# First nine units of a 7-product matrix stage in plain 8-product form, with its preparation rearranged

## The chip, the cores and the metric

One Trainium2 chip, one core. The metric is the time of one execution on the device in microseconds (us). TensorE (PE) multiplies; VectorE (DVE), ScalarE (ACT) and GpSimd (POOL) do elementwise work; SyncE (SP) issues nearly all DMAs of the part that matters here. Each engine runs its own instructions in program order and waits on semaphores for the others.

## The reference, cut to what matters

Attention for 32 heads feeds a mixture of eight experts; its output `x` (2304 tokens, 512 features) goes through a normed gated layer with 1536 hidden columns:

```python
def _moe2_ref(x, w_gate, w_val, w_out, rms_g):
    rms = np.sqrt(np.mean(x * x, axis=-1, keepdims=True) + 1e-06)
    xn = x / rms * rms_g
    g = xn @ w_gate
    silu = g * (1.0 / (1.0 + np.exp(-g)))
    val = xn @ w_val
    return (silu * val @ w_out).astype(np.float32)
```

The change is in the part that computes `silu * val`. The weights of this layer arrive as 64-bit floats.

## The kernel before, in words

Every product of float32 matrices is made of three passes (`PASSES`, L762): each operand is split into a high part, cast by ScalarE to a rounded format, and a low part, the rest, subtracted by VectorE or GpSimd. A product `x @ w` is hi.hi + hi.lo + lo.hi.

**The stages.** Attention comes first, then `moe` (L868): experts s = 0 to 7, each with `gemm1` (L765, eight blocks f) and `gemm2` (L781, four blocks c). Then `glu` (L1245) computes silu(g) times val, and `glu_rest` (L1421) multiplies by `w_out` (the "go" products, L1393).

**The 7-product stage.** The tokens are taken in pairs of groups of 384: p = 0, 1, 2 stands for groups 2p and 2p+1. The weights are taken in 12 blocks f of 128 hidden columns, gate and value together. For one (p, f), called a unit, the 2 x 2 block product (two token groups by gate and value, over two halves of the 512 features) is computed with seven block products in Winograd's form rather than eight: sums of x blocks (S1 to S4) and of weight blocks are made beforehand, and sums of the products afterwards. A block product is six matmuls of 128 x 384 (two 128-row chunks, three passes). Products accumulate in three PSUM banks of the unit, `a`, `b` and `e`; the steps in `glu_step` (L1128) are u1 (copy of a), u2 (b + u1), u3 (b + u1 after the next product was added to b), c21, c12, c22, and then for each token group a sigmoid, `gate` (times g) and `h` (times val), and a store of h (`keep0`, `keep1`). c22, gate2 and h2 are GpSimd's.

**Preparation of a weight block** f: two loads into staging tiles (`w_load`), ten decode steps that turn 64-bit floats to float32 (`decoding`, L1051: VectorE with one ScalarE step), four sums (`w_sum`, GpSimd except for block 1), four casts (`w_cast`, L1097, ScalarE) and four subtractions (`w_rest`, L1102, GpSimd) into one of two buffers `ws0`, `ws1`. **Preparation of the x blocks** of a pair p: two loads from the DRAM array `ytd`, to which the experts' normed outputs are stored, into a staging tile (`glu_load`, L1012; `ringa` for p = 0 and 2, a tile `gx2a` for p = 1), four sums in place (`x_sum`, L1025, VectorE), seven casts (`x_cast`, L1029) and seven subtractions (`x_rest`, L1034) into `gx0a`, `gx0b` and so on.

**What sets the order.** Each engine's order is written out by hand. The first two weight blocks and the x blocks of p = 0 are prepared by `glu_head` (L1170), a generator of which `moe` takes one step after each block of the last experts' products, from the first block of expert 6's `gemm2` on; its instructions stand in each engine's queue between those of the experts. `moe`'s own work in that stretch is: a ReLU per block of `gemm1` on ScalarE (L777) and its residual on VectorE (L778), copies and squares per block of `gemm2` on ScalarE (L796 to L801), sums of squares on VectorE (L802), and `finish` (L813), the norm: a matmul with ones, a square root, a reciprocal (L819) and four multiplications (L822). For expert 7, `finish` is `k.tail`, put into the first unit. From `glu` on, a list `plan` of (due time in products, function) is sorted and emitted: products, unit steps, and the rest of the preparation at `slots`, fixed offsets within each unit (`ONDVE`, `ONPOOL`).

**Addresses.** `glu_first` (L990) opens a pool in the place of the pool that held the weights of the even experts and expert 7's transposed input, in the order ws0, ws1, gx0a, gx0b, ringa; a tile must wait for the last reader of what lay at its address. `glu_second` (L1001) opens the other pool in the place of expert 7's weights and hidden values.

## Time and profile before

| what | value |
|---|---|
| time, median of three runs | 947.37 us (946.16 to 947.95) |
| the profiled execution's own time | 947.75 us |
| its span, first to last instruction | 946.0 us |
| TensorE busy | 857.6 us (91%) |
| VectorE, ScalarE, GpSimd busy | 555.1, 471.8, 554.3 us |
| granted clock of TensorE, mean | 0.97 of full |

The profile takes one execution. Its page shows busy time of each engine, the span in 40 slices, the chain of work that ended last, and groups of instructions; the trace behind it can be asked for stretches of time, waits, single lines and the timeline. In a timeline, "[4.47 <-DMA ringa<-ytd]" means that the engine was idle for 4.47 us before this instruction and that a DMA into ringa ended the wait.

### The profile page before, as it was taken

To read this page: it belongs to the slowest core of one execution; us is meant where nothing else is said; L and a number is where in the kernel's file an instruction comes from. 1 tells how busy PE (TensorE), PEld (TensorE's weight loads), DVE (VectorE), ACT (ScalarE), POOL (GpSimd) and SP (SyncE) were. 2 spreads that over 40 slices of the span, in tenths; PEclk is the share of its full clock that TensorE was granted. 3 is DMA by queue.
4 is the path that set the end of the run, shared out by engine and by line. 5 is a ranking of instruction groups with operands and counts; after the bars stand their busy time and mean duration, and the time that the engine had idled before them with its cause. 6 is when DMAs were issued, how large, how long until landed. Compare 5 with 4: busy or idle time off the path is not lost.

```text
span 946.0 us, 15623 instructions
## 1 busy us (share of the span) xinstructions
PE 857.6 (91%) x5468; PEld 753.7 (80%) x5468; DVE 555.1 (59%) x1179; ACT 471.8 (50%) x1114; POOL 554.3 (59%) x471
## 2 busy tenths in 40 slices
PE   6998989898999999996457899999999999999995
PEld 4676767678899999995457798999999998778884
DVE  5556765645525543466888878888888877700000
ACT  4986969672756555653344333333333443443210
POOL 2002420223686666672845697888888878789541
PEclk9999999998999999998788999999999999999999
DMA  8997775205476565674232041322223278260001
GB/s 266 304 300 221 215 213 169 90 24 173 141 236 196 180 180 180 197 212 135 67 117 102 34 125 64 99 95 102 99 96 126 95 256 295 103 267 34 34 34 37
DMA packets 59452, 139.89 MB, mean 148 GB/s; under 512 B 6960, under 2 KB 24395, under 8 KB 59363
## 3 DMA queue, kind: packets, MB, share of 16 engines
q1 hardware_dynamic: 56403, 129.26, 43.1%
q0 software_dynamic: 2912, 9.46, 2.6%
q8 instruction: 45, 0.74, 0.3%
q14 instruction: 44, 0.36, 0.1%
q10 hardware_dynamic: 48, 0.07, 0.0%
HBM read 103.85 MB, written 34.92 MB: 147 GB/s over the span
## 4 chain that ended last, share of the span: by engine, by line
PE 61%; DVE 20%; ACT 6%; issue 6%; DMA 3%; POOL 2%; SPq 0%; POOLq 0%; ACTq 0%; DVEq 0%
PE go L1393 11%; PE gg L1123 11%; PE g L794 9%; PE g L774 9%; PE pvy L353 5%; PE t L307 5%; PE s L262 4%; DVE raw L1055 4%; DVE raw L1063 2%; PE tl L381 2%; ACT raw L1056 2%; DVE raw L1062 1%; PE sm L275 1%; DVE raw L1061 1%; DVE u L1139 1%
## 5 line engine op out<-in xcount | busy, mean ns | idle before, releaser
L658 POOL TENSOR_TENSOR u<-raw,u 128x1024 fp32r<-128x1024 f32 x64 | 154.4, 2425 | 100.6 <-ACT u L657 100.5
L794 PE MATMUL g<-h,u 128*128 128x256 f32 (+7 forms) x768 | 112.9, 306 | 10.9 <-DVE h L778 6.0
L794 PEld LDWEIGHTS g<-h,u 128*128 128x128 f32 x768 | 107.0, 198 | 13.5 <-DVE h L778 7.6
L774 PE MATMUL g<-xt,u 128*128 128x256 f32 (+7 forms) x768 | 104.3, 295 | 0.0
L774 PEld LDWEIGHTS g<-xt,u 128*128 128x128 f32 x768 | 101.4, 188 | 0.8
L248 DVE CUSTOM_DVE_ANT_0 sc<-s,in 128x128 f32<-128x128 f32 (+3 forms) x128 | 58.1, 490 | 39.8 <-ACT vp L365 13.0
L288 ACT ACTIVATE p<-sc,nm 128x128 f32<-128x128 f32 (+3 forms) x128 | 71.7, 596 | 8.4 <-DVE nm L248 7.7
L235 POOL COPY in<-in 64x64 f32<-64x64 f32 x32 | 8.0, 251 | 115.0 <-PE sm L277 46.2
L1102 POOL TENSOR_TENSOR ws<-raw,ws 128x512 fp32r<-128x512 f32 (+1 forms) x48 | 67.1, 1416 | 6.3 <-ACT ws L1097 6.3
L1123 PE MATMUL gg<-gx1a,ws 128*128 128x384 f32 x288 | 58.8, 347 | 13.1 <-DVE u L1141 13.1
L657 ACT CAST u<-raw 128x1024 fp32r<-128x1024 f32 x64 | 67.6, 1056 | 2.1 <-DMA raw<-in_w 2.1
L340 ACT COPY pt<-t 128x512 f32<-128x512 f32 (+3 forms) x160 | 55.7, 473 | 21.6 <-PE t L307 20.9
L1398 DVE COPY raw<-go 128x256 f32<-128x256 f32 x1 | 0.4, 424 | 110.5 <-ACT raw L1397 110.5
L1123 PEld LDWEIGHTS gg<-gx1a,ws 128*128 128x128 f32 x288 | 51.2, 192 | 16.6 <-DVE u L1141 16.6
L1157 POOL TENSOR_TENSOR h<-u,h 128x384 f32<-128x384 f32 x36 | 45.7, 1271 | 28.8 <-ACT h L1155 28.8
L802 DVE TENSOR_TENSOR sq<-sq,sn 128x256 f32<-128x256 f32 (+6 forms) x21 | 13.9, 664 | 82.4 <-ACT sn L801 82.4
L1123 PE MATMUL gg<-gx0a,ws 128*128 128x384 f32 x288 | 57.3, 340 | 2.9 <-DVE u L1141 2.9
L307 PE MATMUL t<-ident,p 128*128 128x128 f32 x400 | 52.6, 276 | 6.2 <-ACT pt L340 2.6
L1123 PE MATMUL gg<-gx2a,ws 128*128 128x384 f32 x288 | 56.9, 341 | 0.5 <-DVE u L1141 0.5
L1056 ACT ACTIVATE raw<-raw 128x512 f32<-128x512 f32 x36 | 24.3, 674 | 60.9 <-DVE raw L1055 48.7
L1123 PEld LDWEIGHTS gg<-gx0a,ws 128*128 128x128 f32 x288 | 50.6, 190 | 4.5 <-DVE u L1141 4.2
L1155 ACT ACTIVATE h<-u 128x384 f32<-128x384 f32 x36 | 19.0, 527 | 70.6 <-DVE u L1153 70.6
(289 smaller groups left out, 2076.8 us busy)
## 6 DMA issues: line engine op xcount, KB each, us to landing
raw<-in_w SPq DMA_DIRECT2D x64, 512.0 KB, 4.4
hd<-h SPq DMA_DIRECT2D x72, 192.0 KB, 1.8
in<-cumd SPq DMA_DIRECT2D x30, 256.0 KB, 9.8
...
```

Source lines behind the costliest of these rows:

```text
L248: k.nc.vector.tensor_tensor_reduce(out=out, in0=ps, in1=bias, scale=-0.125, scalar=3e38, op0=ALU.add, op1=ALU.min, accum_out=accum)
L288: k.nc.scalar.activation(out, st.s[i, h][:, 0:w], AF.Exp, bias=st.nm[:, n:n + 1], scale=-1.0, accum_out=acc)
L307: nc.tensor.transpose(ps[:, off:off + 128], src[:, 128 * j:128 * j + 128], k.ident)
L340: nc.scalar.copy(b, a)
L353: nc.tensor.matmul(st.y[r, a - 64:512], st.v[:, h, j, :], k.pt[:, h, o:o + S - a], start=j == 0, stop=j == 4)
L657: nc.scalar.copy(w[:, :, 0, :], raw)
L658: nc.gpsimd.tensor_tensor(w[:, :, 1, :], raw, w[:, :, 0, :].bitcast(F32), op=ALU.subtract)
L774: nc.tensor.matmul(ps[:, 0:n], w[:, f % 4, a, 128 * kc:128 * kc + 128], x[b][:, kc, 0:n], start=kc == 0 and i == 0, stop=kc == 3 and i == 2)
L794: nc.tensor.matmul(ps[:, 0:n], w[:, f % 4, a, 128 * c:128 * c + 128], k.h[b][:, f, 0:n], start=f == 0 and i == 0, stop=f == 7 and i == 2)
L1102: k.nc.gpsimd.tensor_tensor(w[:, c, LO, :], src, plain(w[:, c, HI, :]), op=ALU.subtract)
L1123: k.nc.tensor.matmul(k.ps[u, bank], w[:, a, 128 * c:128 * c + 128], x[:, b, GT * c:GT * c + GT], start=j < 3 and c == 0 and n == 0, stop=c ...
L1393: k.nc.tensor.matmul(acc[g][t], c[:, a, cols], w[:, b, :], start=f == 0 and i == 0, stop=f == NF - 1 and i == 2)
```

## The change

The first nine units are computed with eight plain block products (`WHOLE`) into four banks, with no sums; the other 27 keep seven products, in another order (`SEVEN`, `WHENS`), where the last two products of a unit come after the first two of the next. The head prepares only the four x blocks of p = 0 and weight block 0 in plain form, and decodes block 1; the rest moves into the plan. Decoding has four steps instead of five. c22, the weight sums, part of `w_rest` and `wo_split` go to VectorE; the copy p5 goes. `ringa` lies right behind `ws0`, `ws1` at the end; there are three staging tiles for x. The steps of the plan get new due times: the preparation takes the slots `FILL` (VectorE) and `FILLP` (GpSimd) in order.

```diff
@@ -969,12 +969,22 @@
 XB = 2 * GT
 LO, HI = 1, 0
 A11, A12, A22, S1, S2, S3, S4 = range(7)
-PRODUCTS = (("a", A11, 0), ("b", S2, 4), ("e", S1, 3), ("a", A12, 1), ("b", S3, 5), ("e", S4, 2), ("b", A22, 6))
-UNITS = ([(0, 0), (0, 1), (1, 0), (2, 0), (1, 1), (2, 1)] + [(p, f) for f in range(2, NF - 2) for p in range(3)]
+A21 = S1
+PLAIN = ((0, 0), (0, 1), (1, 0), (1, 1), (2, 0), (2, 1), (0, 2), (1, 2), (2, 2))
+UNITS = (list(PLAIN) + [(p, f) for f in range(3, NF - 2) for p in range(3)]
          + [(0, NF - 2), (1, NF - 2), (0, NF - 1), (1, NF - 1), (2, NF - 2), (2, NF - 1)])
...
+WHOLE = tuple((n, *xw) for n, pair in (("c11", ((A11, 0), (A12, 1))), ("c12", ((A11, 3), (A12, 2))),
+                                       ("c21", ((A21, 0), (A22, 1))), ("c22", ((A21, 3), (A22, 2)))) for xw in pair)
+SEVEN = (("a", A11, 0), ("b", S2, 4), ("a", A12, 1), ("e", S1, 3), ("b", S3, 5), ("b", A22, 6), ("e", S4, 2))
+WHENS = ((0, 1, 4, 5, 6, 9, 10), (0, 1, 6, 4, 5, 7, 8))
+NP8 = len(PLAIN)
+START = [8 * u for u in range(NP8)] + [8 * NP8 + 7 * u for u in range(len(UNITS) + 1 - NP8)]
+FILL = ([s + o for s in START[:NP8] for o in (0.65, 1.2, 1.75, 2.2, 3.25, 4.65, 5.2, 5.75, 6.25, 7.25)]
+        + [s + o for s in START[NP8:] for o in (1.3, 1.9, 2.5, 3.65, 4.15)])
+FILLP = [s + o for s in START[:NP8] for o in (0.2, 2.2, 4.2, 6.2)] + [s + o for s in START[NP8:] for o in (0.05, 1.6)]
+STEPS7 = (("u1", 1.05), ("gate1", 5.7), ("u2", 4.6), ("sig1", 5.05), ("u3", 7.1), ("c22", 7.65), ("c21", 10.1),
+          ("sig2", 10.7), ("gate2", 11.45), ("c12", 12.1), ("h2", 12.5), ("h1", 13.25), ("keep1", 13.8), ("keep0", 14.0))
+STEPS8 = (("sig1", 2.05), ("gate1", 2.7), ("h1", 4.1), ("keep0", 4.8), ("sig2", 6.05), ("gate2", 6.7), ("h2", 8.1), ("keep1", 8.8))
...
@@ -989,10 +999,11 @@
 def glu_first(k):
     P = k.gpool
-    k.ws = [glu_tile(k, P, [7, 2, 256], f"ws{n}", F32R) for n in range(2)]
+    k.ws = [glu_tile(k, P, [7, 2, 256], "ws0", F32R)]
+    k.yb = [glu_tile(k, P, [4, XB], "ringa")]
     k.gx = {}
     x_tiles(k, P, 0)
-    k.yb = [glu_tile(k, P, [4, XB], "ringa")]
+    k.ws.append(glu_tile(k, P, [7, 2, 256], "ws1", F32R))
...
@@ -1001,8 +1012,21 @@
 def glu_second(k):
     P = k.hpool
     x_tiles(k, P, 1)
-    k.tmp = [{n: glu_tile(k, P, [GT], f"{n}{i}") for n in ("u1", "p5", "u2", "u3", "h1", "h2")} for i in range(2)]
-    k.yb += [glu_tile(k, P, [4, XB], "gx2a"), k.yb[0]]
+    k.hs = [glu_tile(k, P, [2, GT], f"hs{i}") for i in range(2)]
+    k.yb += [glu_tile(k, P, [4, XB], "tmp"), glu_tile(k, P, [4, XB], "gx2b")]
+    a = glu_tile(k, P, [4, 2, XB], "gx2a", F32R)
+    k.gx[2] = [a[:, n] for n in range(4)]
+
+
+def glu_again(k):
+    b = glu_tile(k, k.hpool, [3, 2, XB], "gx2b", F32R)
+    k.gx[2] += [b[:, n] for n in range(3)]
+    k.yb[2] = k.yb[0]
+
+
+def glu_third(k):
+    t = glu_tile(k, k.hpool, [8, GT], "tmp")
+    k.tmp = [{"u1": t[:, 4 * i], "u2": t[:, 4 * i + 1], "u3": t[:, 4 * i + 2]} for i in range(2)]
...
     def top():
-        V.scalar_tensor_tensor(low, high, 0xC0000000, low, op0=ALU.bitwise_and, op1=ALU.bitwise_or)
-        k.nc.scalar.activation(hf, hf, AF.Abs)
+        V.scalar_tensor_tensor(low, high, 0x80000000, low, op0=ALU.bitwise_and, op1=ALU.bitwise_or)
+        k.nc.scalar.activation(hf, hf, AF.Abs, scale=65536.0)
     return (
         lambda: V.tensor_scalar(low, low, 29, None, op0=ALU.logical_shift_right),
         top,
-        lambda: V.tensor_scalar(hf, hf, TINY, None, op0=ALU.max),
-        lambda: V.tensor_scalar(high, high, 3, 0x3FFFFFFF, op0=ALU.logical_shift_left, op1=ALU.bitwise_and),
-        lambda: V.tensor_tensor(high, high, low, op=ALU.bitwise_or),
+        lambda: V.tensor_scalar(hf, hf, 65536.0 * TINY, None, op0=ALU.max),
+        lambda: V.scalar_tensor_tensor(high, high, 3, low, op0=ALU.logical_shift_left, op1=ALU.bitwise_or),
     )
...
+ORDER = ((0, 0), (0, 1), (1, 0), (1, 1), (0, 2), (0, 3), (1, 2), (1, 3))
+
+
 def w_decode(k, f, n):
-    decoding(k, k.raw[f, n // 5])[n % 5]()
+    m, step = ORDER[n]
+    decoding(k, k.raw[f, m])[step]()
...
-    eng.tensor_tensor(out, a, b, op=ALU.subtract)
+    k.nc.vector.tensor_tensor(out, a, b, op=ALU.subtract)
 def w_piece(k, f, n):
     g, gl, v, vl = w_parts(k, f)
-    c = (slice(0, 2), slice(2, 3), slice(3, 5), slice(5, 7))[n]
...
-    bank, xi, wi = PRODUCTS[j]
-    if j < 3:
+    whole = u < len(PLAIN)
+    bank, xi, wi = (WHOLE if whole else SEVEN)[j]
+    first = (u, bank) not in k.ps
+    if first:
         k.ps[u, bank] = k.psum.tile([128, 512], F32, name=f"gg{k.uid()}", tag="b")[:, 0:GT]
...
+    elif what == "c22":
+        V.tensor_tensor(u3, e, u3, op=add)
+    elif what == "c21":
+        V.tensor_tensor(u1, b, u1, op=add)
+    elif what == "c12":
+        V.tensor_tensor(u2, e, u2, op=add)
...
-        G.tensor_tensor(t["h2"], t["u1"], t["h2"], op=mult)
+        (V if whole else G).tensor_tensor(h2, c21, h2, op=mult)
     elif what == "h2":
-        G.tensor_tensor(t["h2"], t["h2"], t["p5"], op=mult)
+        (V if whole else G).tensor_tensor(h2, c22, h2, op=mult)
...
     dec(5)
     w_cast(k, 0, 0)
-    w_rest(k, 0, 0)
+    yield
+    w_rest(k, 0, 0, G)
     yield
     dec(6)
     yield
...
     dec(7)
...
+    for n in (1, 4):
+        w_cast(k, 0, n)
+        w_rest(k, 0, n, G)
+    yield
+    dec(8)
+    yield
+    dec(9)
+    yield
+    yield
+    x_cast(k, 0, "A11")
+    x_cast(k, 0, "A12")
+    x_rest(k, 0, "A11", V)
+    dec(10)
+    yield
+    x_cast(k, 0, "A21")
+    x_rest(k, 0, "A12", V)
+    x_cast(k, 0, "A22")
+    dec(11, 12)
+    yield
+    x_rest(k, 0, "A21", V)
+    x_rest(k, 0, "A22", G)
+    dec(13)
+    yield
+    dec(14, 15)
...
+        whole = u < len(PLAIN)
+        when = range(8) if whole else WHENS[u == len(UNITS) - 1]
+        for j, at in enumerate(when):
+            add(START[u] + at, glu_product, k, u, j)
+        for what, at in STEPS8 if whole else STEPS7:
...
+            add(START[u] + at, glu_step, k, u, what)
...
+    sums, done = {}, {}
+    for g in (2, 3):
+        add(0.01 * g, glu_load, k, g)
+    for n in (0, 1, 4):
+        t = pfill(0)
+        add(t - 0.1, w_cast, k, 1, n)
+        add(t, w_rest, k, 1, n, G)
+    t = fill(1.9, 5)
+    add(1.6, k.tail)
+    for g in (4, 5):
+        add(8.0 + 0.1 * g, glu_load, k, g)
+    x_rests(1, (("A11", V), ("A12", V), ("A21", V), ("A22", G)), 8.1)
+    load, over, sent = {2: 0.5, 3: 6.5}, {}, {}
+
+    def w_made(f):
+        whole = (0, f) in PLAIN
         for m in range(2):
...
+            add(load[f] + 0.1 * m, w_load, k, f, m)
+        for n in range(8):
+            t = fill(load[f] + 6.0)
+            add(t, w_decode, k, f, n)
+        for n in range(0 if whole else 4):
+            t = fill(t)
+            add(t, w_sum, k, f, n)
+        sent[f] = t + 0.8
+
+    def w_split(f):
+        whole = (0, f) in PLAIN
+        end = last[f - 2] + 1
+        at = max(START[end] + (0.2 if (0, f - 2) in PLAIN else 4.0), sent[f])
+        t = v = at
+        for n, eng in ((0, V), (4, G), (1, V)) if whole else ((0, V), (2, G), (3, G), (1, V)):
+            if eng is V:
+                t = v = fill(v + 0.8)
+            else:
+                t = at = pfill(at + 0.8)
+            add(t - 0.8, w_cast, k, f, n)
+            add(t, w_rest, k, f, n, eng)
+        over[f] = max(at + 1.5, v + 0.8)
+        load[f + 2] = over[f]
+
+    w_made(2)
+    x_rests(2, (("A11", V), ("A12", G), ("A21", V), ("A22", V)), 19.0)
+    w_split(2)
+    w_made(3)
+    x_sums(0, ("S3", "S1", "S2", "S4"), 12.5)
+    x_rests(0, (("S2", G), ("S3", V), ("S4", V)), 12.0)
+    w_split(3)
+    x_sums(1, ("S3", "S1", "S2", "S4"), 24.0)
+    x_rests(1, (("S2", G), ("S3", V), ("S4", V)), 24.0)
+    w_made(4)
+    x_rests(0, (("S1", V),), START[7] + 1.1)
+    x_rests(1, (("S1", G),), START[8] + 1.1)
+    t = done[0, "S1"] + 1.0
+    add(t, glu_again, k)
+    for g in (4, 5):
+        add(t + 0.1 * g, glu_load, k, g)
+    t = done[1, "S1"] + 1.0
+    add(t, glu_third, k)
+    assert t < START[9] + 1.0
+    x_sums(2, ("S3", "S1", "S2", "S4"), done[0, "S1"] + 7.0)
+    x_rests(2, (("S2", V), ("S1", V), ("S3", G), ("S4", V)), START[9] + 1.2)
+    w_split(4)
+    w_made(5)
+    add(130.0, glu_ids, k)
+    add(150.0, glu_turn_ids, k)
...
-    k.nc.gpsimd.tensor_tensor(w[:, LO, :], hf, plain(w[:, HI, :]), op=ALU.subtract)
+    k.nc.vector.tensor_tensor(w[:, LO, :], hf, plain(w[:, HI, :]), op=ALU.subtract)
...
-    add(7 * 33 + 0.6, glu_regions, k, 0)
...
+    add(end - 14 + 3.6, glu_regions, k, 0)
     for n in range(3):
         for g in range(2):
-            add(7 * 33 + 0.7 + 3 * n, h_load, k, g, 4 * n, 4 if n < 2 else 3)
+            add(end - 14 + 3.7 + 1.5 * n, h_load, k, g, 4 * n, 4 if n < 2 else 3)
     for g in range(2):
-        add(7 * 34 + 6.5, h_load, k, g, NF - 1, 1)
-    add(7 * 34 + 0.6, glu_regions, k, 1)
+        add(end - 7 + 7.2, h_load, k, g, NF - 1, 1)
+    add(end - 7 + 3.6, glu_regions, k, 1)
     for f in range(WREADY):
-        add(7 * 34 + 0.9 + 2.2 * f, wo_split, k, f)
+        add(end - 7 + 3.9 + 1.7 * f, wo_split, k, f)
     for n in range(AHEAD):
-        add(7 * 34 - 1.0 + 2.1 * n, glu_split, k, n)
-    add(7 * 35 + 0.6, glu_regions, k, 2)
+        add(end - 7 + 0.5 + 2.3 * n, glu_split, k, n)
+    add(end + 3.6, glu_regions, k, 2)
```

## Rows read from the trace of the kernel before

**Rows 1.** TensorE in the 40 slices of the page, tenths busy (each 23.65 us).

```profile
PE   6998989898999999996457899999999999999995
```

**Rows 2.** Windows (length, busy PE, PEld, DVE, ACT, POOL, clock, DMA share, GB/s).

```profile
437.00:450.00 13.00, 5.58 (x24) 3.88 (x22) 7.16 (x12) 4.27 (x9) 2.04 (x2) 0.73 0.49 164
450.00:460.20 10.20, 10.18 (x75) 10.18 (x76) 9.34 (x7) 5.18 (x10) 10.12 (x7) 0.85 0.48 156
460.20:477.30 17.10, 1.68 (x9) 1.28 (x8) 13.33 (x14) 5.05 (x12) 12.10 (x9) 0.59 0.00 0
477.30:541.20 63.90, 47.20 (x216) 44.04 (x215) 57.09 (x70) 24.76 (x43) 34.52 (x24) 0.87 0.27 94
541.20:781.40 240.20, 229.86 (x1294) 223.95 (x1294) 198.46 (x287) 93.31 (x191) 202.80 (x175) 1.00 0.34 115
781.40:946.00 164.60, 152.17 (x650) 120.91 (x648) 35.49 (x43) 49.20 (x101) 104.23 (x99) 0.99 0.30 114
```

**Rows 3.** TensorE's waits, 438 to 560 (total us, times, longest).

```profile
PE ms L816 <- DVE y L802: 15.4, 1, 15.4
PE gg L1123 <- DVE u L1141: 8.6, 4, 3.6
```

**Rows 4.** Timeline at the last expert (start, us, engine, line).

```profile
428.49 8.64 PE L774 MATMUL g<-xt,u 128*128 128x248 f32 x72
...
431.19 0.36 SPq L1043 DMA_DIRECT2D raw<-in_wv  x1
...
431.75 0.67 ACT L1097 CAST ws<-raw 128x512 fp32r<-128x512 f32 x1 [2.29 <-DVE raw L1063]
431.96 1.81 DVE L819 RECIPROCAL sq<-sq 128x268 f32<-128x268 f32 x1
...
433.81 1.72 DVE L822 SCALAR_TENSOR_TENSOR y<-y,gv,sq 128x268 f32<-128x268 f32 x4
...
437.16 1.31 SPq L1014 DMA_DIRECT2D ringa<-ytd  x2
...
442.27 0.83 ACT L1029 CAST gx0a<-ringa 128x768 fp32r<-128x768 f32 x1 [4.47 <-DMA ringa<-ytd]
443.00 0.37 ACT L777 ACTIVATE h<-g 128x248 fp32r<-128x248 f32 x1
```

**Rows 5.** Timeline of TensorE in the steady stretch, two products each.

```profile
637.04 2.26 PE L1123 MATMUL gg<-gx2a,ws 128*128 128x384 f32 x12
639.13 2.26 PE L1123 MATMUL gg<-gx2b,ws 128*128 128x384 f32 x12
```

**Rows 6.** Window of three units in the steady stretch.

```profile
634.84:658.04 23.20, 22.28 (x127) 21.77 (x127) 19.09 (x29) 8.88 (x18) 20.09 (x17) 1.00 0.29 97
```

**Rows 7.** VectorE lines (duration ns min/median/max, first and last start, forms).

```profile
L1055 DVE SCALAR_TENSOR_TENSOR raw<-raw x36: 678/1146/2803, 423.5 to 821.3; 128x512 uint32<-128x512 uint32 x36
...
L1059 DVE TENSOR_SCALAR raw<-raw x36: 412/707/2020, 423.0 to 820.9; 128x512 uint32<-128x512 uint32 x36
...
L1063 DVE TENSOR_TENSOR raw<-raw x36: 676/1387/2535, 429.2 to 824.7; 128x512 uint32<-128x512 uint32 x36
...
L1034 DVE TENSOR_TENSOR gx1b<-gx2a,gx1b x3: 944/1148/2472, 490.9 to 498.2; 128x768 fp32r<-128x768 f32 x3
...
L1085 DVE TENSOR_TENSOR raw<-raw x2: 419/423/427, 472.6 to 472.9; 128x256 f32<-128x256 f32 x2
...
L1149 DVE TENSOR_TENSOR h<-h,u x36: 557/812/1704, 493.9 to 781.2; 128x384 f32<-128x384 f32 x36
...
L1145 DVE TENSOR_TENSOR h<-gg,h x36: 543/554/559, 490.0 to 779.0; 128x384 f32<-128x384 f32 x36
```

**Rows 8.** GpSimd lines, the same columns.

```profile
L1102 POOL TENSOR_TENSOR ws<-raw,ws x48: 738/1492/1778, 432.5 to 748.6; 128x512 fp32r<-128x512 f32 x36, 128x256 fp32r<-128x256 f32 x12
...
L1157 POOL TENSOR_TENSOR h<-u,h x36: 995/1300/1569, 497.5 to 786.3; 128x384 f32<-128x384 f32 x36
...
L1034 POOL TENSOR_TENSOR gx1a<-gx2a,gx1a x3: 1832/1971/2041, 480.3 to 490.8; 128x768 fp32r<-128x768 f32 x3
```

More of the change, by code (lines that the diff above doesn't have):

```diff
@@ L1130, in glu_step @@
     p, f = UNITS[u]
-    t = k.tmp[u % 2]
-    a, b, e = (k.ps.get((u, n)) for n in "abe")
+    h1, h2 = (k.hs[u % 2][:, n] for n in range(2))
     add, mult = ALU.add, ALU.mult
+    whole = u < len(PLAIN)
+    if whole:
+        c11, c12, c21, c22 = (k.ps.get((u, n)) for n in ("c11", "c12", "c21", "c22"))
+    else:
+        t = k.tmp[u % 2]
+        u1, u2, u3 = t["u1"], t["u2"], t["u3"]
+        c11, b, e = (k.ps.get((u, n)) for n in "abe")
+        c12, c21, c22 = u2, u1, u3
     if what == "u1":
-        nc.scalar.copy(t["u1"], a)
-    elif what == "p5":
-        nc.scalar.copy(t["p5"], e)
+        nc.scalar.copy(u1, c11)
@@ L1165 @@
[L1165 to L1167 removed]
+        nc.sync.dma_start(out=k.hd[2 * p + n, :, f, :], in_=(h1, h2)[n])
 def glu_head(k):
@@ L1250, in add @@
         plan.append((at, len(plan), fn, a))
[L1252 to L1253 removed]
     V, G = k.nc.vector, k.nc.gpsimd
[L1256 removed]
+    last = {}
     for u, (p, f) in enumerate(UNITS):
[L1258 removed]
         last[f] = u
[L1260 to L1263 removed]
@@ L1301, in glu @@
-    glu_second_product(k, add, slots, over)
+        whole = u < len(PLAIN)
+        when = range(8) if whole else WHENS[u == len(UNITS) - 1]
+        for j, at in enumerate(when):
+            add(START[u] + at, glu_product, k, u, j)
+        for what, at in STEPS8 if whole else STEPS7:
+            if u == len(UNITS) - 1:
+                at = {"gate1": 7.7, "sig1": 7.05, "u3": 6.1, "c22": 6.65, "c21": 8.1, "u2": 2.6, "sig2": 8.7, "gate2": 9.45,
+                      "c12": 9.1, "h1": 9.8, "h2": 10.5, "keep0": 10.6, "keep1": 11.5}.get(what, at)
+            add(START[u] + at, glu_step, k, u, what)
@@ new lines, in glu, with fill, pfill, x_rests @@
+    free, pool = list(FILL), list(FILLP)
+    def fill(at, size=1):
+        n = next(i for i, t in enumerate(free) if t >= at)
+        at = free[n]
+        del free[n:n + size]
+        return at
+    def pfill(at):
+        n = next(i for i, t in enumerate(pool) if t >= at)
+        return pool.pop(n)
+    def x_rests(p, blocks, at):
+        for b, eng in blocks:
+            start = max(at, sums.get((p, b), 0.0) + 1.7)
+            t = fill(start, 2) if eng is V else pfill(start)
+            add(max(t - 0.9, sums.get((p, b), 0.0) + 0.3), x_cast, k, p, b)
+            add(t, x_rest, k, p, b, eng)
+            done[p, b] = t
@@ new lines, in x_sums @@
+    def x_sums(p, blocks, at):
+        for b in blocks:
+            t = fill(max([at] + [done.get((p, n), 0.0) + 0.2 for n in ("A11", "A12", "A21", "A22") if p < 2]), 2)
+            add(t, x_sum, k, p, b)
+            sums[p, b] = t
+    sums, done = {}, {}
[9 more added lines that the diff above has]
+        add(8.0 + 0.1 * g, glu_load, k, g)
@@ new lines, in glu @@
+    for g in (4, 5):
[9 more added lines that the diff above has]
+    add(150.0, glu_turn_ids, k)
+    for f in range(5, NF):
+        w_split(f)
+        if f + 1 < NF:
+            w_made(f + 1)
+    glu_second_product(k, add, fill, over)
```

157 lines of the change are left out of this document (33 added, 124 removed).

## The prediction

> **What bounds the kernel now.** I read the page's slices first: TensorE is at nine tenths nearly everywhere, with one hole at slices 18 to 21, where the 7-product stage begins [rows 1]. The windows price it [rows 2]. The last expert's second product stalls (437 to 450: 5.58 us busy of 13). From 460.2 to 477.3 TensorE does 1.68 us of work. Up to 541.2 it is busy 47.2 of 63.9 us; then it runs at 96% until 781.4, and the last stage takes 164.6 us. The waits say on whom [rows 3]: 15.4 us for VectorE's L802, in one piece, and 8.6 us for u3 (L1141). So in the hole the preparation, queued in order on VectorE and ScalarE, sets the pace, and from 541 on TensorE does. The timeline shows the head of that queue [rows 4]: the staging load is issued at 437.16, when the last first-product matmul (428.49 + 8.64) leaves the tile at its address, though SP was free after 431.19; ScalarE then waits 4.47 us for it at x_cast, with the ReLU (443.00) behind.
>
> **A product's price.** Two products start 2.09 us after the two before them [rows 5]: 1.045 us each, 7.32 a unit of seven. Three units, one weight block, take 23.20 us in the steady stretch [rows 6] against 21.95: 0.42 us of stall a unit. u3, which already heads the hole's waits beside L802 [rows 3], has only 1.3 product times between its step and the product that overwrites its bank.
>
> **The change, part by part.**
>
> *Nine plain units.* 9 more products, +9.4 us, certain. In exchange the first units need no sums: the head loses eight weight sums, four x sums, the three S blocks' casts and splits and the second weight block's splits; these come later, as fill, under the plain products.
>
> *Start of the stage.* The new address lies under weights whose last reader is earlier; the load can go at 431.5 instead of 437.2. x_cast now stands behind gemm2's first ScalarE pieces, so nothing queues behind that load. What is late next: w_cast(0, 0) waits for the fourth decode step, now behind the norm of expert 6 (1.81 and 1.72 us on VectorE, to 435.5 [rows 4]). Adding from there the step (0.7), the cast (0.67), the remaining ReLUs and their residuals (0.4 each), four more decode steps (about 0.55) and two casts, I put the last h at 445, an estimate. gemm1 ends at 437.1; gemm2 is 96 matmuls at 0.12 us (8.64 for 72 [rows 4]), 11.5 us. Without waits the stage starts at 448.7; with h at 445, 0.5 us of the first quarter and 8.6 of the others remain: 454, and 1 us for a clock that was at 0.73 in that stretch before [rows 2]: 455. Bounds: 449 and 460, as now. A-block splits need 3 VectorE pieces of 0.95 us between the quarters, and fit. L802 then stands ahead of only two decode steps, and the norm's matmul comes after two products (2.1 us): the 15.4 us wait goes to nothing, bound 0 to 5.
>
> *Loads and queues.* The second staging tile lies where the expert's last weights are, so its two loads wait on SP for gemm2's end, with the weight loads of block 2 behind them; they land some 5 us later (437.16 to 442.27 [rows 4]), and unit 2 needs them 16.7 us after the start: nothing. The third pair waits for the last norm's store, with h stores and weight loads behind; needed 33 us in: nothing. Without the cover each costs its 5 us.
>
> *Plain stretch.* 72 products, 75.2 us. VectorE there, at bare durations, that is the least ones of [rows 7]: 36 unit steps at 0.55, 19 x sums and splits at 0.945, 31 decode steps 16.8, eight weight sums at 0.42, four weight splits 2.2, last norm 3.4: 63.6 us. GpSimd has 11 operations, 18.8 us at [rows 8] (an x split about 2). It fits, at 63.6 plus a fifth of 18.8 (the share found below), 67 of 75; PSUM lets VectorE lag by a dozen products, but by the plan's due times the splits of the second and third block have only 3 to 8 us of slack. Bounds for stalls 0 and 11 (all blocks late); I take 2.5, nearer the fitting sum.
>
> *Seven-product units.* 27, 197.5 us of products. VectorE per three units, bare [rows 7]: six PSUM steps each (9.9), h1 (1.7), eight decode steps (4.4, the new last one priced as L1063), four weight sums (1.7), two splits (1.1): 18.7 us; before it was 15.1 for 28 operations. The rows show what GpSimd adds: 19.09 us busy, 4.0 more than bare, beside 20.09 us of GpSimd [rows 6]: a fifth of it. After the change GpSimd keeps six steps of 1.0 and two splits of 1.49 [rows 8], 9.0 us; a fifth is 1.8. So 20.5 of 21.95 us: VectorE just fits, at 93%. u3 now has two product times, and c12, c21 and c22 are due later still. I take 0.15 us stall a unit, 4 us; bounds 0 and 1.8 a unit (below).
>
> The Trainium skill ("SBUF — State Buffer", Who interferes with whom) says the port shared by VectorE and GpSimd is an exclusive lock, and an operation with two SBUF inputs blocks for the whole of the other's. The trace agrees in kind: L1149 takes 0.557 to 1.704 us, L1145, which reads PSUM, 0.543 to 0.559 [rows 7]. By the rule taken strictly, all GpSimd time falling on VectorE, the total would be rival 3's 953 instead of 901.
>
> *Last stage.* 12 splits of its weights move to VectorE, idle there, and one decode step of five goes; the h loads come 10 products before the end instead of 20. Idle time of TensorE there is 12.4 us [rows 2], mostly the end; bounds -2.5 and +3, I take 0, and 0.5 for the seam between forms. ScalarE's copy of e goes: 9 of 23 us busy [rows 6], off the path.
>
> *Sum.* 455 + 75.2 + 2.5 + 197.5 + 4 + 0.5 = 734.7 against 781.4: -46.7. The profiled execution's own time is 947.75 (span 946.0 and 1.75 around it), 0.4 above the median of 947.37: about **901 us**.
>
> **Rivals.**
> 1. *VectorE binds.* Its waits for ScalarE (gate1, the clamp) eat the 1.4 us that are left; units stay at 23.20/3 = 7.73 and the plain stretch loses 11: 27 x 0.26 + 8.5 = +15.5, 916.5. For: 93% leaves little, and such waits exist now. Against: u3 has more room.
> 2. *The head does not get earlier.* The stage starts at 460 as now, since the decode steps sit between ReLU residuals in order; or L802 queues again, for up to 10 of its 15.4 us: +5 to +15, about 911. Then the new address brought nothing, the load being hidden.
> 3. *Slower: the port.* In the 27 units all GpSimd time falls on VectorE: 18.7 + 9.0 = 27.7 us per three, 9.23 a unit, +47.6; the plain stretch 63.6 + 18.8 = 82.4 against 77.7, +4.7: 953. It decides from 9.19 a unit (7.47 + 46.4/27). Against: before, it would have made 15.1 + 20.1 = 35.2 us where 23.2 were taken [rows 6].
>
> **How the numbers follow.** 0.2% is about what a measurement of this kernel can tell from no change. Forecast 0.58 (own range 888 to 909: start 449, no stalls; or start 458 and 5 more), rival 1 0.22, rival 2 0.13, rival 3 0.07 (0.02 of it within 0.2%, 0.05 slower). Faster 0.93, same 0.02, slower 0.05. The range runs from 889 to 922: below lie 0.03, above the whole of rival 3 and a twentieth from 1 and 2.
>
> **What would show it.** Right: the first L1123-type product near 455, the ninth unit over by 533, units at 7.3 to 7.6 us, last stage from 735; GpSimd under half busy, VectorE near nine tenths. Wrong: the start at 460 or a long wait of the norm's matmul on L802 (rival 2); windows of three units of 23 us or more with waits on u2, u3, c22 (1); 27 us (3). A load waited for on ScalarE near units 2 or 4 would break the queue argument.

## The result, and the profile after

The changed kernel takes **920.11 us** (median of 4 runs, 916.23 to 920.98) against 946.76 for the kernel before (945.99 to 947.95): ratio 0.9709, 95% interval 0.9678 to 0.974, so 26.6 us faster. That lies in the range (889 to 922), 19 us above the forecast of 901. The profiled execution is one of 920.85 us with a span of 918.9. The stage ends that the prediction counted to, in both traces:

| | before | after | difference | forecast |
|---|---|---|---|---|
| last expert's 72 first-product matmuls begin | 428.49 | 447.16 | **+18.67** | 0 |
| from there to the first unit | 31.7 | 26.29 | -5.4 | -5.2 |
| units | 321.2 | 275.06 | -46.1 | -41.5 |
| last stage | 164.6 | 170.39 | **+5.8** | 0 |
| end of the span | 946.0 | 918.9 | -27.1 | -46.7 |

Two lines that the forecast set to zero take back 24.5 of the 51.6 us that the others bring. TensorE in the 40 slices of the changed kernel's page (22.97 us each, counted from 0) answers to [rows 1]:

```profile
PE   6199998998999999999899999999999999799995
```

The hole at slices 18 to 21 is gone, and a new one stands in slice 1 (23 to 46 us), in attention, which the diff does not touch. A smaller dent is in slice 34, in the last stage (experiment 6). The windows of the changed kernel (columns as in [rows 2]): the last expert's second product, the nine plain units, the 27 units of seven, the last stage:

```profile
455.80:473.45 17.65, 14.86 (x96) 13.61 (x96) 10.78 (x18) 8.11 (x19) 4.63 (x4) 0.81 0.20 71
473.45:548.78 75.33, 75.33 (x436) 75.29 (x435) 67.79 (x107) 33.33 (x57) 17.12 (x12) 1.00 0.51 169
548.78:748.51 199.73, 198.53 (x1137) 196.62 (x1137) 169.15 (x308) 71.14 (x138) 85.63 (x73) 1.00 0.33 117
748.51:918.90 170.39, 154.04 (x649) 120.35 (x648) 36.98 (x46) 50.98 (x104) 89.58 (x89) 0.98 0.30 113
```

The plain stretch has no idle TensorE at all, the units of seven 1.2 us of it, and the granted clock is 1.00 in both, where the stretch up to 541 had 0.87 [rows 2]. TensorE's waits from 455 on, against the 15.4 and 8.6 us of [rows 3]:

```profile
PE g L794 <- ACT h L777: 1.9, 2, 1.1
PE go L1465 <- ACT ws L1456: 1.5, 2, 0.8
...
PE gg L1157 <- DVE tmp L1177: 0.6, 2, 0.3
PE gg L1157 <- DVE tmp L1179: 0.6, 1, 0.6
```

The norm's matmul no longer waits; u3 (L1179) costs 0.6 us in all. What is left stands in the last expert (L794) and in the last stage (L1465).

**The new hole.** The timeline of SP's queue early in the changed kernel, and then in the kernel before:

```profile
17.11 1.07 SPq L228 DMA_DIRECT2D vp<-in_v  x2
18.22 0.43 SPq L161 DMA_DIRECT2D gv<-in_rms_g  x1
18.75 0.39 SPq L164 DMA_DIRECT2D tokd<-oob  x1
19.34 10.00 SPq L166 DMA_DIRECT2D xs<-zrow  x8
29.44 1.25 SPq L213 DMA_DIRECT2D in<-in_q  x1
```

```profile
17.36 1.06 SPq L228 DMA_DIRECT2D vp<-in_v  x2
18.53 0.36 SPq L213 DMA_DIRECT2D in<-in_q  x1
18.99 0.38 SPq L214 DMA_DIRECT2D in<-in_k  x1
...
25.76 2.08 SPq L166 DMA_DIRECT2D xs<-zrow  x2
...
33.87 0.93 SPq L166 DMA_DIRECT2D xs<-zrow  x2
```

The eight zero fills of `xs` (771 KB each, 16.1 us from issue to landing) used to go two at a time between the loads of the next pairs. Now all eight go ahead of the third pair's q, k and bias. (The expectation of experiment 1 says the second pair's; by these rows it is the third's.) They are issued 11 us later and share the DMA engines with 6.2 MB of zeros: k, issued at 30.80, is waited for until 45.92. TensorE is 9.41 us busy in the window from 18 to 46 us, and 27.15 in the same window of the kernel before: 17.7 us go there. The DMA engines are full in both windows (DMA share 1.03 and 1.00, 314 and 303 GB/s), so the zeros stand in the place of loads and not in idle time. The waits of the changed kernel in its first 70 us name the loads:

```profile
DVE sc L248 <- DMA in<-cumd: 23.7, 3, 19.7
...
PE s L262 <- DMA in<-in_k: 17.7, 1, 17.7
```

The cause is a name. Attention places its fills by a module-level pair, and the change defines a module-level list of the same name further down; attention runs later and reads the list, so the fills are due at 0.65 + 1.2n instead of 16 + 5n:

```
FILL = (16.0, 5.0)
...
            add(FILL[0] + FILL[1] * n, prefill, k, n)
...
FILL = ([s + o for s in START[:NP8] for o in (0.65, 1.2, 1.75, ...
```

### The profile page after: what moved, and what is told of

Read it like the earlier page. It is cut to its first block, busy times and chain, and to the rows that moved or that the text cites. A ratio compares the mean times of both kernels' runs of the same rounds, so it can differ in the third digit from the quotient of the medians.

```text
span 918.9 us, 15493 instructions
## 1 busy us (share of the span) xinstructions
PE 857.4 (93%) x5522; PEld 757.4 (82%) x5522; DVE 516.9 (56%) x1223; ACT 454.8 (49%) x1069; POOL 385.0 (42%) x334
## 4 chain that ended last, share of the span: by engine, by line
PE 40%; issue 4%; DVE 3%; POOL 2%; DMA 1%; ACT 1%; SPq 0%; POOLq 0%; ACTq 0%; DVEq 0%
PE gg L1157 27%; PE go L1465 11%; PE g L794 1%; POOL ws L1457 1%; DMA raw<-in_wo 1%; DMA ringa<-ytd 1%; DVE raw L1090 0%; POOL ringa L1457 0%; DVE raw L1089 0%; DVE gx1a L1393 0%; ACT raw L1084 0%; DVE raw L1083 0%; DVE ringa L1050 0%; ACT gx1a L1392 0%; DVE h L778 0%
## 5 line engine op out<-in xcount | busy, mean ns | idle before, releaser
L794 PE MATMUL g<-h,u 128*128 128x256 f32 (+7 forms) x768 | 111.2, 303 | 5.1 <-ACT h L777 1.9
L794 PEld LDWEIGHTS g<-h,u 128*128 128x128 f32 x768 | 105.7, 196 | 7.2 <-DVE h L778 2.9
L288 ACT ACTIVATE p<-sc,nm 128x128 f32<-128x128 f32 (+3 forms) x128 | 71.6, 592 | 26.8 <-DVE nm L248 26.5
L1195 POOL TENSOR_TENSOR hs<-tmp,hs 128x384 f32<-128x384 f32 x27 | 30.3, 1123 | 106.3 <-ACT hs L1193 106.3
L262 PE MATMUL s<-in 64*128 64x128 f32 (+3 forms) x256 | 52.5, 507 | 18.3 <-DMA in<-in_k 17.7
L1157 PE MATMUL gg<-gx2a,ws 128*128 128x384 f32 x360 | 67.4, 335 | 0.6 <-DVE tmp L1179 0.6
L1157 PE MATMUL gg<-gx0a,ws 128*128 128x384 f32 x360 | 67.7, 336 | 0.0
L1157 PE MATMUL gg<-gx1a,ws 128*128 128x384 f32 x360 | 67.1, 335 | 0.0
L1157 PEld LDWEIGHTS gg<-gx2a,ws 128*128 128x128 f32 x360 | 62.8, 188 | 0.9 <-DVE tmp L1179 0.9
L1157 PEld LDWEIGHTS gg<-gx0a,ws 128*128 128x128 f32 x360 | 63.1, 188 | 0.0
L1157 PEld LDWEIGHTS gg<-gx1a,ws 128*128 128x128 f32 x360 | 62.7, 188 | 0.0
L802 DVE TENSOR_TENSOR sq<-sq,sn 128x256 f32<-128x256 f32 (+6 forms) x21 | 14.0, 669 | 83.6 <-ACT sn L801 83.6
L1084 ACT ACTIVATE raw<-raw 128x512 f32<-128x512 f32 x36 | 24.4, 677 | 62.6 <-DVE raw L1083 35.7
## 6 DMA issues: line engine op xcount, KB each, us to landing
xs<-zrow SPq DMA_DIRECT2D x8, 771.0 KB, 16.1
```

The lines of the kernel that those rows point to most:

```text
L262: nc.tensor.matmul(ps[h], st.q[r, 128 * i:128 * i + 128], st.k[r, 0:w], start=True, stop=False)
L288: k.nc.scalar.activation(out, st.s[i, h][:, 0:w], AF.Exp, bias=st.nm[:, n:n + 1], scale=-1.0, accum_out=acc)
L794: nc.tensor.matmul(ps[:, 0:n], w[:, f % 4, a, 128 * c:128 * c + 128], k.h[b][:, f, 0:n], start=f == 0 and i == 0, stop=f == 7 and i == 2)
L1157: k.nc.tensor.matmul(k.ps[u, bank], w[:, a, 128 * c:128 * c + 128], x[:, b, GT * c:GT * c + GT], start=first and c == 0 and n == 0, stop=c ...
L1195: (V if whole else G).tensor_tensor(h2, c21, h2, op=mult)
```

## The experiments

The runs were made in four groups. The second ran on a chip on which the kernel before takes 936.40 us and the last expert comes some 11 us sooner; across groups, compare ratios to the kernel before, or lengths of stages. "Head" is from the start of the last expert's 72 matmuls to the first unit.

**1. Names apart (e1_names_apart).**

```diff
-FILL = ([s + o for s in START[:NP8] ...
+FILLV = ([s + o for s in START[:NP8] ...
...
-    free, pool = list(FILL), list(FILLP)
+    free, pool = list(FILLV), list(FILLP)
```

> The new list of VectorE due times gets a name of its own (FILLV), so that attention reads its old FILL = (16.0, 5.0) again; nothing else differs from the changed kernel. Theory (the shared name moved the eight zero fills of attention ahead of the second pair's loads, and that costs the 18.65 us by which the last expert's first matmul is late: 447.16 against 428.49): 920.1 - 18.7 = 901.5 us, and that matmul at 428.5 again. Rival (the late part comes from something else of the change, as the other address of the staging tile): about 920 us, the matmul still at 447.

Measured: **900.46 us** (897.21 to 902.08, 5 runs), ratio 0.9508 (0.9487 to 0.9529). The 72 matmuls start at 427.48, head 26.05, units 275.01, last stage 169.96. The theory holds: these are the missing 19 us. The same kernel once more in the third group (e9_names_apart_again):

> The run with names apart once more, beside the best version on one chip, as the measure for it and for the runs of the second group, which were made on another chip than the first. Theory and rival alike: a ratio of 0.950 to 0.951 to the kernel before, as in the first group.

Measured: 901.26 us beside 947.67, ratio 0.951 (0.9494 to 0.9526).

**2. The early fills alone, in the kernel before (e2_before_early_fills).**

```diff
-FILL = (16.0, 5.0)
+FILL = (0.65, 1.2)
```

> The kernel before with FILL = (0.65, 1.2) in attention: the zero fills at the due times that the changed kernel gives them by accident, and nothing else of the change. Theory of the shared name: 946.8 + 18.7 = 965.4 us, with the whole of the difference before the last expert. Rival (something else of the change): no difference, 946.8 us; a value between them says that part of the 18.65 us has another cause.

Measured: 964.68 us (963.1 to 966.51), ratio 1.0198 (1.018 to 1.0215), 18.15 us more. In its profile, of the shortest execution, the 72 matmuls start at 443.95, 15.5 us late, the time from there to the last stage (352.75) is that of the kernel before (352.94), and its page shows the same hole in slice 1 (TensorE in the slices; the second hole is the old one at the units' start):

```profile
PE   6299898988999999998647798999999999999995
```

So one line of numbers, without anything else of the change, costs nearly all of what the changed kernel lost.

**3. The staging tile at its old address (e3_old_address)**, on top of names apart:

```diff
-    k.ws = [glu_tile(k, P, [7, 2, 256], "ws0", F32R)]
-    k.yb = [glu_tile(k, P, [4, XB], "ringa")]
+    k.ws = [glu_tile(k, P, [7, 2, 256], f"ws{n}", F32R) for n in range(2)]
     k.gx = {}
     x_tiles(k, P, 0)
-    k.ws.append(glu_tile(k, P, [7, 2, 256], "ws1", F32R))
+    k.yb = [glu_tile(k, P, [4, XB], "ringa")]
```

> As the run with names apart, but the staging tile (ringa) is laid out behind the x tiles again, at its address of before, so its load has to wait for the last expert's first product. Theory (the load lands at some 442 in the time of the kernel before, and the first x_cast now stands behind the second product's first pieces at some 445 to 446, so the load is hidden): within 1 us of the run with names apart, 901 to 902.5. Rival (the new address is what brings the head forward): x_cast waits some 4 to 5 us with ScalarE behind it, so about 906.

Measured: 900.41 us, ratio 0.951 (0.9497 to 0.9523): no difference. The load goes at 435.81 instead of 430.93, and the first x_cast, at 444.16, waits for nothing. The head is 26.85 us, where runs with the same head code and the new address show 26.05 to 26.91 (experiments 1 and 6). The new address brings nothing here; what is left to bring the head's gain is the rearranged preparation.

**4. Consecutive products (e4_consecutive)**, on top of names apart:

```diff
-WHENS = ((0, 1, 4, 5, 6, 9, 10), (0, 1, 6, 4, 5, 7, 8))
+WHENS = ((0, 1, 2, 3, 4, 5, 6), (0, 1, 6, 4, 5, 7, 8))
...
-STEPS7 = (("u1", 1.05), ("gate1", 5.7), ("u2", 4.6), ("sig1", 5.05), ("u3", 7.1), ("c22", 7.65), ...
+STEPS7 = (("u1", 1.05), ("gate1", 3.7), ("u2", 2.6), ("sig1", 3.05), ("u3", 4.6), ("c22", 5.15), ...
```

> As the run with names apart, but the seven products of a unit stand one behind the other (0 to 6) instead of interleaved with the next unit's (0, 1, 4, 5, 6, 9, 10), with the steps due accordingly; work and engines are the same. Theory (in the 7-product stretch it is the room between u3 and the product that overwrites its bank, two products instead of one or none, that takes the stall away): TensorE waits for u3 in each unit, at least the step's 0.55 us and two semaphores, about 0.9 us, up to some 2 us where fill work of VectorE stands ahead of it: 26 units by 0.9 to 2 = 23 to 52 us, so 924 to 952 us, the wait named u3's line. Rival (the gain per unit came from taking work off GpSimd alone, the order doesn't matter): 900 to 905 us.

Measured: 941.3 us beside 936.4, ratio 1.0062 (1.0039 to 1.0085), some 51 us above names apart; units 328.35 us against 275.01. The waits of TensorE from 530 to 800 in this run, and a stretch of its timeline:

```profile
PE gg L1157 <- DVE tmp L1179: 22.1, 26, 2.5
PE gg L1157 <- DVE tmp L1177: 13.7, 17, 1.5
```

```profile
587.16 0.55 DVE L1177 TENSOR_TENSOR tmp<-gg,tmp 128x384 f32<-128x384 f32 x1
587.63 0.68 DVE L1083 SCALAR_TENSOR_TENSOR raw<-raw 128x512 uint32<-128x512 uint32 x1
587.76 1.31 PE L1157 MATMUL gg<-gx1b,ws 128*128 128x384 f32 x6 [1.25 <-DVE tmp L1177]
...
589.17 0.56 DVE L1179 TENSOR_TENSOR tmp<-gg,tmp 128x384 f32<-128x384 f32 x1
...
589.78 2.29 PE L1157 MATMUL gg<-gx1a,ws 128*128 128x384 f32 x6 [0.72 <-DVE tmp L1179]
```

u3 (L1179) is waited for in 26 of 26 units, as the theory has it, but its 22.1 us lie just under the theory's lower end of 23; with u2 (L1177), waited for in 17 units, and with longer matmuls the total comes out at its upper end. The room that the interleaved order gives these steps is worth more than all that names apart gains on the kernel before (46 us). The waits alone are 35.8 us. The rest is matmuls that take longer: in the window of the 27 units TensorE is 216.49 us busy, 17.8 more than the 198.71 that the same 1136 take in names apart (its window stands under experiment 5).

```profile
517.70:770.73 253.03, 216.49 (x1136) 200.50 (x1136) 200.01 (x308) 70.63 (x139) 89.89 (x73) 0.97 0.27 93
```

**5. GpSimd's gates on VectorE (e5_gates_on_vectore)**, on top of names apart:

```diff
-        (V if whole else G).tensor_tensor(h2, c21, h2, op=mult)
+        V.tensor_tensor(h2, c21, h2, op=mult)
...
-        (V if whole else G).tensor_tensor(h2, c22, h2, op=mult)
+        V.tensor_tensor(h2, c22, h2, op=mult)
```

> As the run with names apart, but gate2 and h2 of the 27 seven-product units are on VectorE too, as they are in the plain units, so GpSimd keeps only two splits of a weight block there. By the prediction's count VectorE's bare work goes from 18.7 to 22.0 us per three units, with a fifth of GpSimd's remaining 3.0 us 22.6, against 21.95 of TensorE. Theory (VectorE at 88 to 93% just fits and has no room for six more steps): units at 7.5 to 7.8 us instead of 7.35, +5 to +12, 905 to 912 us. Rival 1 (GpSimd's share costs VectorE far more than a fifth, so taking it away pays for the steps): no change or a gain, 895 to 900. Rival 2 (VectorE falls behind until its splits are late in every block): +20 or more.

Measured: 893.39 us beside 936.4, ratio 0.9548 (0.9529 to 0.9568), about 3.6 us above names apart; plain and seven-product units together 279.69, 4.7 more. A unit of seven takes 7.57 us (204.28 / 27, window below) against 7.39: the theory's lower end for a unit. The time lies between rival 1 (no change) and the theory's lower end (+5). The 27 units' window of names apart, then of this run:

```profile
528.90:728.54 199.64, 198.71 (x1136) 196.77 (x1135) 169.55 (x308) 71.18 (x138) 85.58 (x73) 1.00 0.34 117
```

```profile
516.90:721.18 204.28, 200.14 (x1136) 196.57 (x1135) 182.59 (x359) 71.41 (x138) 28.70 (x21) 1.00 0.33 115
```

The 52 moved steps last 30.3 us on VectorE in this window. The durations of its other instructions add up to about 10 us less than in names apart, while GpSimd lost 56.9 us of work. So some 0.18 of GpSimd's time lay on VectorE (an estimate from these sums), near the prediction's fifth. The moved steps cost VectorE about three times what they free. That it is only 13.0 us longer busy is also due to instructions that overlap (see below on VectorE's count).

**6. The output weights' splits back on GpSimd (e6_wo_on_gpsimd)**, on top of names apart:

```diff
-    k.nc.vector.tensor_tensor(w[:, LO, :], hf, plain(w[:, HI, :]), op=ALU.subtract)
+    k.nc.gpsimd.tensor_tensor(w[:, LO, :], hf, plain(w[:, HI, :]), op=ALU.subtract)
```

> As the run with names apart, but the twelve residual splits of the output weights (wo_split) are on GpSimd again. Theory (the last stage grew from 164.6 to 170.4 us because this split joined the serial chain of decode steps on VectorE: every second iteration takes 5.92 us there against some 5.1 to 5.2 before): the last stage back to 165 to 167 us, so 3 to 6 us less than the run with names apart, 896 to 898. Rival 1 (it grew because the loads of h and the first splits start later): no change, 901.5. Rival 2 (GpSimd is the slower engine for it and the ring's residuals queue behind): 1 to 4 us more.

Measured: **895.04 us** (six runs, ratio 0.9455, 0.9443 to 0.9468), 5.4 below names apart. Its profiled execution is one of 900.60 us that came to the last expert 4.3 us later than names apart did, so stage lengths are what to read from it: head 26.91, units 274.41, last stage **165.58** instead of 169.96. The theory holds, with the time 1 us below its range. The chain that this split had joined, one iteration of the loop in the last stage of names apart (one block f for two token groups; the expectations call it two f):

```profile
757.05 1.10 POOL L1457 TENSOR_TENSOR ringa<-gx0a,ringa 128x384 fp32r<-128x384 f32 x1 [3.66 <-ACT ringa L1456]
757.20 1.23 DVE L1087 TENSOR_SCALAR raw<-raw 128x512 uint32<-128x512 uint32 x1
...
758.10 1.20 POOL L1457 TENSOR_TENSOR ringa<-gx0b,ringa 128x384 fp32r<-128x384 f32 x1
...
758.46 1.39 DVE L1083 SCALAR_TENSOR_TENSOR raw<-raw 128x512 uint32<-128x512 uint32 x1
759.93 0.67 ACT L1084 ACTIVATE raw<-raw 128x512 f32<-128x512 f32 x1 [2.55 <-issue]
760.63 0.43 DVE L1089 TENSOR_SCALAR raw<-raw 128x512 f32<-128x512 f32 x1 [0.79 <-ACT raw L1084]
761.10 0.69 DVE L1090 SCALAR_TENSOR_TENSOR raw<-raw 128x512 uint32<-128x512 uint32 x1
761.82 0.65 ACT L1392 CAST gx1b<-raw 128x512 fp32r<-128x512 f32 x1 [1.22 <-DVE raw L1090]
762.38 0.51 ACT L1456 CAST ringa<-gx0a 128x384 fp32r<-128x384 f32 x1
762.51 0.69 DVE L1393 TENSOR_TENSOR gx1b<-raw,gx1b 128x512 fp32r<-128x512 f32 x1 [0.72 <-ACT gx1b L1392]
...
762.94 0.73 PE L1465 MATMUL go<-gx1b,ringa 128*128 128x512 f32 x2 [0.74 <-ACT ringa L1456]
...
763.12 1.23 DVE L1087 TENSOR_SCALAR raw<-raw 128x512 uint32<-128x512 uint32 x1
```

VectorE's and ScalarE's steps on `raw` and the split (L1393) follow one another: from L1087 to the next L1087 5.92 us, where TensorE's 18 matmuls take 4.2. In the kernel before, without the split on VectorE, an iteration takes 5.15 us from its first decode step to the next one:

```profile
805.45 0.42 DVE L1059 TENSOR_SCALAR raw<-raw 128x512 uint32<-128x512 uint32 x1
...
810.60 0.42 DVE L1059 TENSOR_SCALAR raw<-raw 128x512 uint32<-128x512 uint32 x1
```

Two links of the chain in names apart are stretched besides: L1087 takes 1.23 us and L1083 1.39 beside GpSimd's two subtractions of the ring (L1457), where the median of the changed kernel's 36 L1087 is 0.42 and L1083 takes 0.68 in the rows of experiment 4. So about 1.5 us of the chain come from running beside GpSimd. That was so in the kernel before as well (L1062 with 1.13 us, L1063 with 1.39), so it does not explain the growth. VectorE is busy for only 36.98 of 170.39 us (last stage of the changed kernel) and still sets the pace. The ring's cast (L1456) that TensorE needs stands on ScalarE behind the cast (L1392) that waits for the chain.

**7. Issued an iteration later (e6c_wo_deferred)**, on top of experiment 6:

```diff
-            wo_split(k, f + WREADY)
-            if f + WREADY + 4 < NF:
-                wo_load(k, f + WREADY + 4)
         if n + AHEAD < len(k.seq):
             glu_split(k, n + AHEAD)
+        if n < 24 and g == 0 and 1 <= f and f - 1 + WREADY < NF:
+            wo_split(k, f - 1 + WREADY)
+            if f - 1 + WREADY + 4 < NF:
+                wo_load(k, f - 1 + WREADY + 4)
```

> As the run with the output weights' splits on GpSimd, but in the last stage a block's cast and split (wo_split) and the next load are issued one iteration later, behind the two casts of the ring, so ScalarE does not hold the ring's casts back while VectorE still decodes. Theory (an iteration of two f is a chain of decode steps on VectorE, their Abs and the cast on ScalarE, and the ring's casts queued behind that cast; the chain and not any engine's work sets 5 to 5.9 us where TensorE needs 4.2): iterations of 4.4 to 4.7 us, 2 to 4 us less than that run, 891 to 893. Rival (GpSimd's three operations of some 1.5 us per iteration are what binds): no change, 895.

Measured: 888.43 us beside 936.4, ratio 0.9495 (0.9479 to 0.9511); last stage 169.3, 3.7 longer than in experiment 6. A miss, of theory and rival. Rows of this run's waits and of its timeline, from the last stage, show why:

```profile
DVE raw L1087 <- DMA raw<-in_wo: 5.6, 1, 5.6
```

```profile
737.45 1.01 POOL L1457 TENSOR_TENSOR ws<-gx0a,ws 128x384 fp32r<-128x384 f32 x1 [1.77 <-ACT ws L1456]
737.47 1.54 DVE L1090 SCALAR_TENSOR_TENSOR raw<-raw 128x512 uint32<-128x512 uint32 x1
738.41 1.47 POOL L1457 TENSOR_TENSOR ringa<-gx0b,ringa 128x384 fp32r<-128x384 f32 x1
```

The load, moved with the split, comes late once (5.6 us). Then the ring's casts stand behind the Abs (L1084) instead of behind the cast, and the decode step L1090 too falls beside GpSimd's subtractions: it takes 1.54 us there, 0.69 in the rows of names apart under experiment 6. The iteration is 5.66 us. So ScalarE's new order did not shorten it here. The order and the later load were changed together, and no run tells them apart.

**8. The head (e7_head)**, on top of names apart:

```diff
-    dec(4)
-    yield
-    dec(5)
+    dec(4, 5)
+    yield
     w_cast(k, 0, 0)
...
     dec(7)
+    yield
+    yield
     for n in (1, 4):
         w_cast(k, 0, n)
         w_rest(k, 0, n, G)
     yield
-    dec(8)
-    yield
-    dec(9)
-    yield
     yield
...
-    dec(10)
+    dec(8, 9, 10)
```

> As the run with names apart, but in the preparation under the last expert the fourth step of the first weight half's decode goes ahead of the norm of expert 6, and the casts (1, 4) of the first block and the first two decode steps of the second block go two to four places later, behind the ReLUs. Theory (ScalarE waits 5.37 us at w_cast for the decode step behind the norm, the last expert's ReLUs and so the second product stand behind it; the second product's 96 matmuls need 11 us and end 17 us after the first product's end): the stage starts 3 to 5 us earlier and the end follows, 895.5 to 897.5 us. Rival 1 (VectorE's residuals stand behind the norm all the same): 0 to 1 us. Rival 2 (VectorE is full in the plain stretch and its splits come late instead, so that the start is given back there): about 900.

Measured: 884.2 us beside 936.4, ratio 0.9444 (0.9428 to 0.946): about 6 us below names apart, a little more than the theory's 3 to 5. The timeline of the changed kernel at the last expert's second product:

```profile
454.12 0.69 DVE L1090 SCALAR_TENSOR_TENSOR raw<-raw 128x512 uint32<-128x512 uint32 x1
454.84 0.65 ACT L1129 CAST ws<-raw 128x512 fp32r<-128x512 f32 x1 [5.37 <-DVE raw L1090]
455.40 0.91 ACT L777 ACTIVATE h<-g 128x248 fp32r<-128x248 f32 x3
...
462.37 11.25 PE L794 MATMUL g<-h,u 128*128 128x248 f32 x75 [0.81 <-ACT h L777]
```

And the timeline of this run:

```profile
420.10 0.69 DVE L1090 SCALAR_TENSOR_TENSOR raw<-raw 128x512 uint32<-128x512 uint32 x1
420.82 0.66 ACT L1129 CAST ws<-raw 128x512 fp32r<-128x512 f32 x1 [1.67 <-DVE raw L1090]
...
425.30 11.52 PE L794 MATMUL g<-h,u 128*128 128x248 f32 x96
```

ScalarE waits 1.67 us instead of 5.37, all 96 matmuls run in one piece, and the head is 19.82 us instead of 26.05. The units give back 1.2 of it (276.2). The edit moves the fourth decode step ahead of the norm and other casts and steps behind the ReLUs; which of the two brings how much was not run.

**9. Together (e8_best)**: the edits of 1, 6 and 8.

> The three edits together: names apart, the output weights' splits on GpSimd, the preparation under the last expert as in the run of the head. Theory (the head's 5 to 6 us and the last stage's 4.4 to 4.8 us lie in different stages and add up): 10 to 11 us less than the run with names apart on the same chip, a ratio to the kernel before of 0.939 to 0.941, head (last expert's second chunk of the first product to the first product of the units) 19.8 us, last stage 165 to 166 us. Rival (the earlier start is given back in the units or the last stage, where something else is then late): 5 us less or below, a ratio of 0.945 or more.

Measured: **890.0 us** (888.31 to 892.83) beside 947.67, ratio **0.9396** (0.9375 to 0.9417), 11.3 below names apart in the same group. Head 19.83, units 274.87, last stage 165.57: the gains lie in different stages and add up. This version beats both kernels.

**10. The old address there (e10_best_old_address)**, the edit of experiment 3 on the best version.

> As the best version, but with the staging tile (ringa) at its address of before. In the best version the first x_cast stands at 440.29, with the last expert's first product over at 436.5; at the old address the load goes only then and lands some 5.1 us later (437.16 to 442.27 in the kernel before), at 441.6. Theory (the new address brings nothing as long as the head is late, and begins to pay where it is early): x_cast waits 1 to 1.5 us for the load, the units start 0.5 to 1.5 us later (head 20.3 to 21.3 instead of 19.83 us), a ratio of 0.940 to 0.942. Rival (hidden here as well): head 19.8 us, no wait, 0.9396.

Measured: 889.73 us beside 946.45, ratio 0.9403 (0.9385 to 0.9421). The wait is there, as the timeline of this run shows, but not its price:

```profile
440.59 1.57 ACT L1054 CAST gx0a<-ringa 128x768 fp32r<-128x768 f32 x2 [1.13 <-DMA ringa<-ytd]
```

ScalarE has 1.13 us to spare there: the head is 19.83 us again. The theory's wait came, but the rival's head and ratio hold. Whether the address pays with a head shorter still was not tried.

## Why the prediction was right, and where it was wrong

The direction, the main reason and the range held. The number did not, and two steps failed. That the range held is luck in part: the forecast's own range ended at 909, and 920 lies in the stretch that was added for rivals 1 and 2, neither of which came about.

**The step that failed: the work ahead of the stage taken as unchanged.** The sum set out from "gemm1 ends at 437.1" and counted to 734.7. It ends at 455.8, 18.7 us later, with nothing of the stage to blame. The diff held the cause, a second definition of `FILL` at module level, and the part-by-part costing priced what the new list places and not who else reads the name. No rival had it either: "slower" was the port alone. Experiments 1 and 2 show it from both sides, 900.46 without the clash and +18.15 with the clash alone. The prediction's 901 is close to what the change does without it, but this too is partly luck: the last stage came out 5.8 us longer than forecast and the stretch before it 4.9 us shorter.

**The second: the last stage at 0, bounds -2.5 and +3.** It measured +5.8. The step said that the splits "move to VectorE, idle there". Idle in share, but they joined a serial chain whose length is the iteration; experiment 6 returns 4.4 us of stage and 5.4 of time. The 1.0 us by which its 165.58 still exceeds 164.6 was not traced; the later h loads are a candidate that no run separates.

**Right, step by step.** *Start*: from the 72 matmuls 26.29 us, forecast 26.5 (455 less 428.49). The h row that gates it came at 462.35, by 18.67 earlier in the old time 443.7, against an estimate of 445, and from there to the first unit 11.1 us passed against 10, so two errors of about 1 us cancel. The cast behind the norm was the thing that is late next, as said; experiment 8, which takes it from there with other steps, gains 6 us. *The new address*: the load goes early as told, but experiments 3 and 10 show that this brings nothing; the prediction had given this only as a part of its second rival. *Plain stretch*: 75.33 us, forecast 75.2 + 2.5; VectorE 67.79 busy, forecast 67 (a sum of durations, which in fact add up to 73; that they overlap makes up for it). *Units of seven*: 199.73 with the seam, forecast 202; stall 0.08 us a unit (2.23 over the products' 197.5, 27 units) against 0.15. *Waits*: L802 none, u3 0.6 us. *Norm, loads, queues*: TensorE waits for none of them.

From the 72 matmuls to the last stage it took 4.9 us less than forecast, nearly all of it stalls. With that, 901.0 - 4.9 + 18.7 + 5.8 = 920.6, against 920.11 measured.

**VectorE was counted at 93% and is at 88%.** Three units of the steady stretch (columns as before):

```profile
635.47:657.32 21.85, 21.85 (x127) 21.85 (x127) 19.16 (x37) 7.50 (x15) 9.48 (x8) 1.00 0.30 103
```

19.2 us busy, where the sum had 18.7 bare and 1.8 for GpSimd, 20.5. As a sum of durations that was right: the 36 instructions that begin in this window add up to 20.7 us. But together they cover only 18.9, since many overlap: in the rows of experiment 4, L1177 begins at 587.16 and takes 0.55, to 587.71, and the next step begins at 587.63. In experiment 5 VectorE's durations add up to 22.8 us per three units, more than TensorE's 21.95, and cover 20.3, so the six steps more still fit.

**The rivals.** *VectorE binds*: not at 88%, and hardly with the gates on it too (+4.7 us). *The head does not get earlier*: it did, by 5.4 us. *The port*: its price of 953 is refuted for the units, where about a fifth of GpSimd's time falls on VectorE (experiment 5). Where the two meet, single steps do get longer: L1090, with two inputs, takes 1.54 us instead of 0.69 beside two subtractions of GpSimd (experiment 7). The Trainium skill ("SBUF — State Buffer", Who interferes with whom) says that an instruction of VectorE with two SBUF inputs contends with a reading GpSimd; the trace agrees in these rows. That all of GpSimd's time would fall on VectorE, as the rival counted, it does not bear out.
